# A small product pass whose first matmuls are cut in halves for two of four row tiles, and whose copies out of PSUM are cut in two

## The chip, the cores and the metric

The kernel runs on one core of a Trainium2 chip. The metric is the device time in microseconds of one execution, lower is better. TensorE (PE in the profile; PEld are its weight loads), VectorE (DVE), ScalarE (ACT), GpSimd (POOL) and the DMA queues run side by side and wait for each other through semaphores. TensorE writes its results into PSUM, which has eight banks of 512 float32 values per partition; VectorE and ScalarE read them there.

## The reference

All in float32, with a batch of 8, 4224 rows and 192 channels:

```python
w = softmax(weight, axis=-1)                    # 8 heads x 7 taps
y = sum over k of w[head, k] * x[s + k - 6]     # causal depthwise convolution, 24 channels a head
mu, var = mean and variance of y over its 192 channels
xn = (y - mu) / sqrt(var + 1e-6) * g_ln
out = y + relu(xn @ w_ch1) @ w_ch2              # 192 -> 768 -> 192
```

The scaling by 1/sqrt(var) is positive, so the kernel moves it behind both matmuls, and the subtraction of the mean and the factor g_ln are worked into `w_ch1` once.

## The kernel before

The rows are cut into 18 groups. A group is at most 128 partitions times 16 rows (`J` = 16). Groups 3 to 17 (15 of them) go through `up_mixed` (first matmul) and then `down_fast` (second matmul); the earlier, smaller ones take other paths that the change leaves as they are. Every engine's instructions are issued in the order in which the code stands (`tc.manual_schedule()`); the semaphore waits follow from the tiles that an instruction reads and writes.

The first matmul is a matrix product in Strassen's manner (Winograd's form): seven products of quarter matrices in place of eight. It is made in two passes, which split the hidden columns: `one` takes one of the three blocks of 128 columns in each half (`Pass(PAIR, FC, X, Y)`, the small pass, `self.n` = 1), `two` takes the other two (`self.n` = 2). Each pass makes the seven products in this order, alternating between two sets of four PSUM banks, X and Y: X, Y, X, Y, X, Y, X. Some products add to what the set already holds (`first=False`), and after most products the set is read out before the next product goes into it.

One product is made by `rows_of_tiles`. The transposed activations lie so that 32 partitions hold 32 channels of one of four row tiles `q` (`NQ` = 4). A matmul of tile `q` uses 32 rows of the array, `32q` to `32q+31`, with 128 weight columns and 256 moving columns (8 row indices `j` times 32), and writes bank `q` of the set. In the small pass a product is 3 channel blocks `c` times 4 tiles `q`: 12 matmuls, written `q` inside `c`. The trace holds two records for each float32 matmul, and as many for its weights, so a product of the small pass has 24 matmul records. Its set holds 4 banks with 256 columns each in use: a readout of it is a 128x1024 operation.

The readout of a set is `evict` (a copy by ScalarE, or a Relu for the last product) or `close`. `close` with a `part` copies the set into a spare place through `evict` and then has a DMA with addition (`add_by_dma`, issued on POOL) add it to its target. In the small pass the ScalarE reads out after each of the seven products: `evict` into `c11`, `close` into the spare `two.c12[:, 0:1]`, `evict` into `c21`, `evict` into `c22`, `close` into `two.c12[:, 1:2]`, `close` into `two.c22[:, 0:1]`, and the Relu into `c12`. Before the change each is one instruction (line 651). In the last group (17, `last`) `evict` already cuts it: ScalarE takes banks 0 and 1, VectorE banks 2 and 3 (lines 642 to 650).

Of the kernel before, what the change touches and what calls it, by code (L numbers as in the profile page):

```python
# [10 lines left out]
AF = mybir.ActivationFunctionType  # L11
# [5 lines left out]
def kernel(  # L17
# [29 lines left out]
    nc = tc.nc  # L47
# [4 lines left out]
    P = 128  # L52
    Q = 64
    C = 32
# [8 lines left out]
    NQ = P // C  # L63
# [20 lines left out]
    HJ = J // 2  # L84
# [35 lines left out]
    def take_bank():  # L120
        i = turn[0] % 8
        turn[0] = i + 1
        return all_banks[:, i]

    def take_set():
        i = (turn[0] + 3) // 4 * 4 % 8
        turn[0] = i + 4
        return all_banks[:, i : i + 4]
# [393 lines left out]
            return  # L522
        nc.scalar.activation(dst, src, AF.Relu)  # L523

    def rows_of_tiles(banks, left, right, first=True, last=True, split=False):


        chunks, w = right.shape[2] // P, left.shape[1] * left.shape[3]
        for c in range(left.shape[2]):
            for i in range(chunks):  # L530
                for q in range(NQ):
                    rows = slice(C * q, C * q + C)
                    nc.tensor.matmul(  # L533
                        banks[:, q, i * w : i * w + w], right[rows, c, P * i : P * i + P],
                        left[rows, :, c, :], start=(first and c == 0 and i == 0),
                        stop=(last and c == left.shape[2] - 1), skip_group_check=split,
                    )

    def between(g, f):

# [12 lines left out]
    def up(g):  # L553


        n = groups[g][2]
        hidden_tile(g)
        for f in range(NF):
            banks = take_set()
            rows_of_tiles(banks, yt[g][:, 0:n], w1[:, :, f * P : f * P + P])  # L560
            evict_up(g, f, banks[:, :, 0 : n * C])
            if g == 0 and f == 0:
                first_tap(1, heads=(0, H // 2))
            elif g == 0 and f == 1:
                copies_of_w1(1, [(q, 1) for q in range(NQ)])
                scale_power(words_2[2])
            elif g == 0 and f < 4:
                first_tap(1, heads=(2 * f, 2 * f + 2))
            between(g, f)
# [16 lines left out]
    def quarters_of_y(g):  # L586
        if width(g) == C:
            cuts = [(slice(HJ * h, HJ * h + HJ), slice(0, C)) for h in range(2)]
        else:
            cuts = [(slice(0, J), slice(T * h, T * h + T)) for h in range(2)]  # L590
        return [yt[g][:, js, CH * k : CH * k + CH, ts] for js, ts in cuts for k in range(2)]
# [19 lines left out]
    def up_mixed(g, ahead, pending):  # L611
# [3 lines left out]
        last = g + 1 == NG  # L615
# [3 lines left out]
        a11, a12, a21, a22 = quarters_of_y(g)  # L619
# [3 lines left out]
        class Pass:  # L623
# [6 lines left out]
                    for h in range(2)  # L630
                ]

            def product(self, to, left, right, first=True, end=True):
                rows_of_tiles(to, left, right, first, end, True)

            def seen(self, banks, f=None):
                src = banks[:, :, 0 : self.n * W] if f is None else banks[:, :, W * f : W * f + W]
# [2 lines left out]
            def evict(self, banks, dst, relu=False, f=None):  # L640
                src = self.seen(banks, f)
                if last and self.n == 1:
                    near, far = [[v[:, :, q : q + 2] for v in (dst, src)] for q in (0, 2)]
                    if relu:
                        nc.scalar.activation(*near, AF.Relu)
                        nc.vector.tensor_scalar_max(*far, 0.0)
                    else:
                        nc.scalar.copy(*near)
                        nc.vector.tensor_copy(*far)
                    return  # L650
                nc.scalar.activation(dst, src, AF.Relu) if relu else nc.scalar.copy(dst, src)  # L651

            def close(self, c, banks, part=None, f=None):

# [25 lines left out]
        X, Y = take_set(), take_set()  # L680
        one, two = Pass(PAIR, FC, X, Y), Pass(0, PAIR, Y, X)
        p = one
        p.product(X, a11, p.b11, True, False)
        p.evict(X, p.c11)
        p.product(Y, a12, p.b21)
        p.close(p.c11, Y, two.c12[:, 0:1])
# [14 lines left out]
        p = two  # L701
# [52 lines left out]
        if last:  # L754

            n = J - fast[g]
# [249 lines left out]
    for g in range(NG):  # L1006
        mixed, last = g in MIXED, g + 1 == NG
        if g + 2 < NG and g not in (1, 2, 3):
            load_x(g + 2)
        if mixed:  # L1010
            work = up_mixed(g, ahead(g), pending)
            pending = iter(())
        else:
            up(g)
            work = []
# [47 lines left out]
        if last:  # L1063
# [4 lines left out]
            for j in range(fast[g], groups[g][2]):  # L1068
                rows = take_bank()[:, 0:D]
# [36 lines left out]
```

## Time and profile before

| | |
|---|---|
| median of 3 runs | 957.89 us (957.74 to 960.14) |
| span of the profiled execution, first to last instruction | 954.6 us |
| PE busy | 946.8 us (99%) |
| DVE busy | 894.2 us (94%) |
| ACT busy | 694.8 us (73%) |
| POOL busy | 341.8 us (36%) |
| granted TensorE clock | 9 (90% or more) in all 40 slices |
| first matmul of a whole group to first matmul of its `down_fast` | 27.96 us in 12 of the 15 groups |

The time of an execution is a few microseconds longer than its span. A line of groups of instructions gives the source line, the engine, the operation, what it writes and reads, the tile shapes, the count, the busy time and the mean length of one, then the idle time of the engine in front of them and what ended it. A line of the timeline gives the start in us from the start of the span, the length of the stretch, and in brackets the idle time before it with its releaser. Matmul records are pipelined: their lengths overlap, so PE counts as busy even while the rate at which matmuls start has dropped.

### The profile page before, as it was taken

To read this page: it belongs to the slowest core of one execution; us is meant where nothing else is said; L and a number is where in the kernel's file an instruction comes from. 1 tells how busy PE (TensorE), PEld (TensorE's weight loads), DVE (VectorE), ACT (ScalarE), POOL (GpSimd) and SP (SyncE) were. 2 spreads that over 40 slices of the span, in tenths; PEclk is the share of its full clock that TensorE was granted. 3 is DMA by queue.
4 is the path that set the end of the run, shared out by engine and by line. 5 is a ranking of instruction groups with operands and counts; after the bars stand their busy time and mean duration, and the time that the engine had idled before them with its cause. 6 is when DMAs were issued, how large, how long until landed. Compare 5 with 4: busy or idle time off the path is not lost.

```text
span 954.6 us, 37896 instructions
## 1 busy us (share of the span) xinstructions
PE 946.8 (99%) x16858; PEld 734.5 (77%) x16858; DVE 894.2 (94%) x1496; ACT 694.8 (73%) x1166; POOL 341.8 (36%) x474
## 2 busy tenths in 40 slices
PE   8999999999999999999999999999999999999998
PEld 7998896877869687786958778695867769586787
DVE  8999999999999999999999999999999999999867
ACT  7764678596877959687796968779695877967362
POOL 1158422613145141533227141452316232261330
PEclk9999999999999999999999999999999999999999
DMA  8359589689696988979697897969889697778261
GB/s 206 111 151 218 110 233 269 122 188 226 130 273 131 251 158 185 221 130 278 126 252 152 199 215 128 277 133 249 158 198 206 124 275 134 174 135 141 40 122 68
DMA packets 39832, 169.34 MB, mean 177 GB/s; under 512 B 4469, under 2 KB 8182, under 8 KB 33655
## 3 DMA queue, kind: packets, MB, share of 16 engines
q0 software_dynamic: 32864, 106.77, 60.2%
q1 hardware_dynamic: 6800, 60.16, 17.4%
q8 instruction: 132, 2.16, 0.9%
q14 instruction: 30, 0.25, 0.1%
q10 hardware_dynamic: 6, 0.00, 0.0%
HBM read 38.93 MB, written 50.33 MB: 94 GB/s over the span
## 4 chain that ended last, share of the span: by engine, by line
PE 96%; DMA 1%; POOL 1%; ACT 1%; issue 0%; DVE 0%; ACTq 0%; POOLq 0%
PE ps L533 46%; PE ps L850 44%; PE ps L787 4%; PE ps L367 1%; DMA room<-room 1%; DMA out_dram<-y 1%; PE ps L326 1%; ACT room L651 0%; POOL room L609 0%; POOL d L460 0%; ACT y L380 0%; POOL r L483 0%; POOL d L478 0%; POOL d L479 0%; PE ps L335 0%
## 5 line engine op out<-in xcount | busy, mean ns | idle before, releaser
L417 DVE SCALAR_TENSOR_TENSOR y<-xg,taps,y 128x384 f32<-128x384 f32 (+3 forms) x720 | 364.8, 583 | 2.6 <-DMA y<-room 1.4
L850 PE MATMUL ps<-room,w2sums 128*32 128x256 f32 (+2 forms) x4608 | 246.6, 371 | 0.0
L533 PE MATMUL ps<-yt,w 32*128 32x256 f32 (+2 forms) x4104 | 234.7, 378 | 1.0 <-ACT room L523 0.5
L533 PEld LDWEIGHTS ps<-yt,w 32*128 32x128 f32 x4104 | 204.2, 185 | 26.3 <-issue 8.7
L651 ACT COPY room<-ps 128x1024 f32<-128x1024 f32 (+1 forms) x129 | 169.0, 1310 | 74.5 <-PE ps L533 73.5
L850 PEld LDWEIGHTS ps<-room,w2sums 128*32 128x32 f32 x4608 | 149.3, 110 | 91.5 <-ACT room L664 5.3
L850 PE MATMUL ps<-room,w 128*32 128x256 f32 (+2 forms) x3456 | 188.9, 371 | 0.0
L817 DVE TENSOR_TENSOR room<-room 128x1024 f32<-128x1024 f32 (+2 forms) x147 | 161.2, 1170 | 22.6 <-PE ps L850 16.0
L850 PEld LDWEIGHTS ps<-room,w 128*32 128x32 f32 x3456 | 110.7, 110 | 70.3 <-DVE room L657 5.0
L533 PE MATMUL ps<-ysums,w1sums 32*128 32x256 f32 x2160 | 124.9, 379 | 0.2 <-issue 0.2
L533 PEld LDWEIGHTS ps<-ysums,w1sums 32*128 32x128 f32 x2160 | 109.5, 185 | 10.5 <-ACT room L651 3.3
L940 POOL DMA_DIRECT2D out_dram<-ot x69 | 59.0, 942 | 155.6 <-ACT ot L929 102.5
L409 POOL DMA_DIRECT2D y<-tb x59 | 52.5, 1386 | 153.5 <-ACT room L856 110.1
L856 ACT COPY cs<-ps 128x256 f32<-128x256 f32 (+2 forms) x192 | 70.1, 367 | 45.2 <-PE ps L850 45.2
L664 ACT ACTIVATE room<-room 128x1024 f32<-128x1024 f32 (+1 forms) x89 | 92.5, 1072 | 1.7 <-DMA room<-parts_cs 0.9
L929 ACT ACTIVATE ot<-ot,r 128x192 f32<-128x192 f32 x224 | 90.9, 464 | 0.0
L380 ACT ACTIVATE y<-xg,taps 128x384 f32<-128x384 f32 (+3 forms) x141 | 73.0, 607 | 1.0 <-DMA out_dram<-y 0.7
L448 DVE BATCH_NORM_STATS2 st<-y 128x6 f32<-128x192 f32 x264 | 70.1, 344 | 0.0
L856 ACT COPY room<-ps 128x256 f32<-128x256 f32 (+2 forms) x96 | 35.5, 370 | 45.8 <-PE ps L850 43.8
L398 ACT ACTIVATE tb<-xg,taps 128x384 f32<-128x384 f32 (+1 forms) x120 | 66.1, 628 | 0.0
L533 PE MATMUL ps<-yt,w1sums 32*128 32x256 f32 x1080 | 65.2, 380 | 0.6 <-ACT room L651 0.6
L533 PE MATMUL ps<-ysums,w 32*128 32x256 f32 x1080 | 64.5, 376 | 0.0
(119 smaller groups left out, 924.8 us busy)
## 6 DMA issues: line engine op xcount, KB each, us to landing
xg<-in_x_dram SPq DMA_DIRECT2D x14, 2112.0 KB, 16.4
room<-room POOLq DMA_DIRECT2D x45, 512.0 KB, 5.1
out_dram<-ot POOLq DMA_DIRECT2D x59, 384.0 KB, 9.6
y<-tb POOLq DMA_DIRECT2D x58, 384.0 KB, 8.4
out_dram<-y SPq DMA_DIRECT2D x13, 1536.0 KB, 8.8
room<-parts_cs POOLq DMA_DIRECT2D x28, 512.0 KB, 6.7
room<-parts_tb POOLq DMA_DIRECT2D x14, 1024.0 KB, 7.6
xg<-in_x_dram POOLq DMA_DIRECT2D x1, 2112.0 KB, 13.8
```

What stands on the lines that cost most here:

```text
L380: nc.scalar.mul(y[g][:, 0:n, cs], xg[g][:, 0:n, cs], taps[:, h, 0:1])
L398: nc.scalar.mul(tb[g][:, 0:n, cs], xg[g][:, 1 : 1 + n, cs], taps[:, h, 1:2])
L417: nc.vector.scalar_tensor_tensor(out=y[g][:, 0:n, cs], in0=t[:, k : k + n, cs], scalar=taps[:, h, k : k + 1], in1=y[g][:, 0:n, cs], op0=AL ...
L448: nc.vector.bn_stats(out=sums[g][:, j, :], in_=y[g][:, j, :])
L533: nc.tensor.matmul(banks[:, q, i * w : i * w + w], right[rows, c, P * i : P * i + P], left[rows, :, c, :], start=(first and c == 0 and i = ...
L651: nc.scalar.activation(dst, src, AF.Relu) if relu else nc.scalar.copy(dst, src)
L664: nc.scalar.activation(c, c, AF.Relu)
L817: nc.vector.tensor_tensor(a[:, *dst, f], a[:, *left, f], a[:, *right, f], op=op)
L850: nc.tensor.matmul(dst[C * q : C * q + C, 0:w], right[:, f, C * c : C * c + C], left[:, f, q], start=(first and f == PAIR), stop=(f == PAI ...
L856: nc.scalar.copy(to[:, c], dst[:, 0:w].rearrange("p (j t) -> p j t", t=t))
L929: nc.scalar.mul(ots[g][:, j, :], ots[g][:, j, :], rstd[g][:, j : j + 1])
L940: nc.gpsimd.dma_start(out=rows[:, d0:d1], in_=src[:, d0:d1], accum_op=ALU.add)
```

## The change

In all groups from 3 on but the last, the first product of the small pass (`X`, from `a11`) is issued with `lead` = 4: for row tiles 0 and 1 a matmul over the first 4 of the 8 `j` (128 of 256 columns) of channel block 0 goes ahead of everything; then the loops run as before, with the tiles 0 and 1 of channel block 0 taking only the other 128 columns. Later channel blocks and products are issued as before. In the small pass each copy of a set that is not a Relu becomes two copies of two banks each (128x512 twice instead of 128x1024). The Relu copy, the large pass and the last group stay as they are.

```diff
-    def rows_of_tiles(banks, left, right, first=True, last=True, split=False):
+    def rows_of_tiles(banks, left, right, first=True, last=True, split=False, lead=0):
 
-        chunks, w = right.shape[2] // P, left.shape[1] * left.shape[3]
+        chunks, n, t = right.shape[2] // P, left.shape[1], left.shape[3]
+        w = n * t
+
+        def one(c, i, q, j1, j2, start):
+            rows = slice(C * q, C * q + C)
+            nc.tensor.matmul(
+                banks[:, q, i * w + j1 * t : i * w + j2 * t], right[rows, c, P * i : P * i + P],
+                left[rows, j1:j2, c, :], start=start,
+                stop=(last and c == left.shape[2] - 1), skip_group_check=split,
+            )
+
+        for q in range(NQ // 2 if lead else 0):
+            one(0, 0, q, 0, lead, first)
         for c in range(left.shape[2]):
             for i in range(chunks):
                 for q in range(NQ):
-                    rows = slice(C * q, C * q + C)
-                    nc.tensor.matmul(
-                        banks[:, q, i * w : i * w + w], right[rows, c, P * i : P * i + P],
-                        left[rows, :, c, :], start=(first and c == 0 and i == 0),
-                        stop=(last and c == left.shape[2] - 1), skip_group_check=split,
-                    )
+                    begun = lead if c == i == 0 and q < NQ // 2 else 0
+                    one(c, i, q, begun, n, first and c == 0 and i == 0 and not begun)
...
-                nc.scalar.activation(dst, src, AF.Relu) if relu else nc.scalar.copy(dst, src)
+                halves = [slice(0, 2), slice(2, NQ)] if self.n == 1 and not relu else [slice(0, NQ)]
+                for qs in halves:
+                    to, of = dst[:, :, qs], src[:, :, qs]
+                    nc.scalar.activation(to, of, AF.Relu) if relu else nc.scalar.copy(to, of)
...
-        p.product(X, a11, p.b11, True, False)
+        p.product(X, a11, p.b11, True, False, 0 if last else HJ // 2)
```

More of the change, by code (lines that the diff above doesn't have):

```diff
@@ L631, in __init__, with product @@
                 ]
-            def product(self, to, left, right, first=True, end=True):
-                rows_of_tiles(to, left, right, first, end, True)
+            def product(self, to, left, right, first=True, end=True, lead=0):
+                rows_of_tiles(to, left, right, first, end, True, lead)
             def seen(self, banks, f=None):
```

## The prediction

> **What bounds the kernel now.** I began with the page's first part and its chain of work: PE is never free.
>
> ```profile
> PE 946.8 (99%) x16858; PEld 734.5 (77%) x16858; DVE 894.2 (94%) x1496; ACT 694.8 (73%) x1166; POOL 341.8 (36%) x474
> ...
> PE 96%; DMA 1%; POOL 1%; ACT 1%; issue 0%; DVE 0%; ACTq 0%; POOLq 0%
> ```
>
> So only what lets matmuls start sooner can shorten the run, and the page cannot show where that is: records overlap, so a late start hides in a busy PE. The weight loads tell. Their timeline in the small pass of a whole group (the pass that begins at 228.41):
>
> ```profile
> 228.41 2.47 PEld L533 LDWEIGHTS ps<-yt,w 32*128 32x128 f32 x48 [0.41 <-issue]
> 231.12 1.18 PEld L533 LDWEIGHTS ps<-ysums,w1sums 32*128 32x128 f32 x24 [0.24 <-ACT room L651]
> 232.48 1.21 PEld L533 LDWEIGHTS ps<-ysums,w1sums 32*128 32x128 f32 x24 [0.18 <-issue]
> 233.83 1.18 PEld L533 LDWEIGHTS ps<-ysums,w 32*128 32x128 f32 x24
> 235.26 1.18 PEld L533 LDWEIGHTS ps<-yt,w1sums 32*128 32x128 f32 x24 [0.26 <-ACT room L651]
> 236.61 1.21 PEld L533 LDWEIGHTS ps<-yt,w 32*128 32x128 f32 x24 [0.17 <-issue]
> 238.03 2.04 PEld L533 LDWEIGHTS ps<-yt,w 32*128 32x128 f32 x40 [0.22 <-ACT room L651]
> ```
>
> From the third product on, the loads of nearly every product start after a pause, and where a releaser is named it is ScalarE's copy of line 651. What that costs, I read from the same seven products of the last group, whose readouts are already cut by bank pair (ScalarE one pair, VectorE the other). Timelines of PE, first the whole group, then the last group, from the pass's first matmul to a product in the middle of the large pass:
>
> ```profile
> 228.41 2.87 PE L533 MATMUL ps<-yt,w 32*128 32x256 f32 x48
> ...
> 243.31 1.90 PE L533 MATMUL ps<-ysums,w1sums 32*128 32x256 f32 x32
> ```
> ```profile
> 894.29 2.87 PE L533 MATMUL ps<-yt,w 32*128 32x256 f32 x48
> ...
> 899.58 1.47 PE L533 MATMUL ps<-ysums,w 32*128 32x256 f32 x24
> 900.87 1.47 PE L533 MATMUL ps<-yt,w1sums 32*128 32x256 f32 x24
> ...
> 908.64 2.55 PE L533 MATMUL ps<-ysums,w1sums 32*128 32x256 f32 x44
> ```
>
> 243.31 − 228.41 = 14.90 us against 908.64 − 894.29 = 14.35 us: **0.55 us are lost in a whole group's small pass.** 14 groups give 7.7 us, 0.8% of the run; that is all that can be won. The undisturbed pace is 900.87 − 899.58 = 1.29 us a product, six steps of 0.216 us in which the four row tiles each run one record.
>
> Why the pass loses it, from ScalarE's timeline in the same stretch:
>
> ```profile
> 230.06 1.01 ACT L651 COPY room<-ps 128x1024 f32<-128x1024 f32 x1 [1.14 <-PE ps L533]
> 231.35 1.01 ACT L651 COPY room<-ps 128x1024 f32<-128x1024 f32 x1 [0.28 <-PE ps L533]
> 232.77 1.01 ACT L651 COPY room<-ps 128x1024 f32<-128x1024 f32 x1 [0.40 <-PE ps L533]
> ```
>
> Call S the start of a product's last step. A record lasts 0.37 us (two products, 228.41 to 231.28) and the copy of the second starts 0.07 later, at 231.35: the copy starts at S + 0.44. It ends at S + 1.45, and the weights go in 0.05 later (231.07 to 231.12), at S + 1.51. The set is wanted again after one product on the other set, so its first matmul should run at S + 0.216 + 1.295 = S + 1.51, but the weights must come first: a tile's first load needs about 0.10 us that is otherwise hidden (after a pause a step takes 0.32 instead of 0.216). The pass is therefore 0.11 us too slow at every wait for a copy. ScalarE itself has room: it idles 0.3 to 0.5 us before every copy. It is the latency of one copy that binds.
>
> **The change, part by part.**
>
> *The copies.* Six copies of 128x1024 per group become twelve of 128x512, 84 more instructions. Both forms are in the trace:
>
> ```profile
> L651 ACT COPY room<-ps 128x1024 f32<-128x1024 f32 x84 | 85.1, 1013 | 42.2 <-PE ps L533 42.2
> L648 ACT COPY room<-ps 128x512 f32<-128x512 f32 x6 | 3.5, 586 | 4.7 <-PE ps L533 4.7
> ```
>
> Two halves take 2 × 0.586 = 1.17 us, unless they overlap. Back-to-back copies do: two of 128x1024 in one stretch take 1.93 us and not 2.03, 0.10 less. So the second half ends 0.586 − 0.10 + 0.586 = 1.07 us after the first begins, 0.06 later than the one copy did; without overlap 0.16 later. I take the overlap, since those two stand on the same engine, line and set. The pair fills 1.07 of each 1.295 us product, so the engine's queue does not run over.
>
> *The waits.* Tiles 0 and 1 now wait for the first half alone, ready at S + 0.44 + 0.59 + 0.05 = S + 1.08 against the S + 1.40 that would be in time: they never wait. Tiles 2 and 3 wait for the second half: S + 0.44 + 1.07 + 0.05 = S + 1.56, matmul at S + 1.67, wanted at S + 1.51. If all four tiles finish together, tiles 2 and 3 lose 0.16 us, once. From then on they run 0.16 us behind the other pair, so at the next sets the first half starts that much ahead of their own end, the second half finds itself in time (1.67 − 0.16 = 1.51), and nothing more is lost. Behind a tile-2 wait on PE's queue stand the next channel block's matmuls of tiles 0 and 1; these already have two records each, 0.43 us, in hand when the wait is reached, more than 0.16.
>
> *The lead.* Four short matmuls of 128 columns in place of two of 256: eight records and loads in place of four. The warm-up matmuls at the start, 128 columns with 128 weight columns, give their price: 28 records in 3.39 us, about 0.11 each, against 0.108 for half a step. Tiles 0 and 1 so lose 4 × 0.111 − 0.432 = 0.01 us, and they have time. What the lead does to tiles 2 and 3 depends on whether PE lets them past the four short matmuls that stand ahead of them. If it does, they start at once and lose the 0.16 us above; if it does not and holds them for two short records, they start 0.22 us late and lose nothing later (0.22 > 0.16). The nearest row says it does:
>
> ```profile
> 228.41 0.71 PE L533 MATMUL ps<-yt,w 32*128 32x256 f32 x8
> ```
>
> The narrower timeline (to 228.72) has only four records here, the next four follow 0.32 us after. Two records of one matmul cannot run in one tile at once, so these four are the first records of four tiles, and the second records, earlier in the program, were overtaken.
>
> The Trainium skill ("TensorE: Matmul & The Clock Gate", Part 3, "What overlaps and what doesn't") says the contrary: matmuls start in strict program order. By that rule tiles 2 and 3 would wait for the short records of tiles 0 and 1, the pass would lose about 0.45 us, and the sum would be near 956.5. The start of four tiles together speaks against it.
>
> *The rest, at nothing.* `close`'s DMA additions wait for the second half, 0.06 us more; they are read about ten us later (issued 232.67, the Relu on `c11` at 247.9). VectorE must keep up with a shorter group: it idles 0.86 us before line 657 until PE's product is done (253.99), more than the gain. Should that cover go, PE would wait at the `down_fast` that follows. SP's queue gets nothing new.
>
> **The sum.** Loss per pass after: 0.16 (tiles pass) to 0.22 (tiles held) us; the calculation for 0.16 closes without a margin, so I take 0.19. Gain 0.55 − 0.19 = 0.36 us × 14 = 5.0 us. The first of the 14 passes (117.20) has another stall of some 0.4 us in its fourth product with no copy behind it, which may swallow its share: −0.2. 4.8 us off the span of 954.6 gives 949.8; the median stands 3.3 above that span, so **953.1 us**. Bounds of the likeliest case: 0.10 us of loss gives 6.3 (951.6); no overlap of the halves, 0.26 of loss, gives 4.0 (953.9).
>
> **The rivals.**
>
> 1. *Slower: the pairs do not come apart.* If PE's queue, standing at tile 2's wait, also stops tiles 0 and 1, every set waits for the second half, which ends 0.06 (overlapped) to 0.16 us (not) later than the one copy, and the 0.22 us of the lead is paid on top. A wait that comes late for X leaves the next one, for Y, time to spare, so three of the six count: 0.22 + 3 × 0.16 = 0.70 us a pass, or 0.22 + 3 × 0.26 = 1.00, against 0.55: 0.15 to 0.45 us more, × 14 = 2.1 to 6.3 us, 960.0 to 964.2. It decides once the loss exceeds 0.55 us a pass. Against it: the overtaking above. For it: no row shows tiles 0.16 us apart.
> 2. *The lead is dear.* If short records cost a whole load (185 ns in the page's group of loads) and not 111, tiles 0 and 1 lose 4 × (0.185 − 0.108) = 0.31 us at once and, with the 0.16 of the other pair, the pass 0.47: gain 0.08 × 14 = 1.1 us, 956.8. The warm-up rows speak against it, but they used the whole array.
> 3. *No difference: the time comes back elsewhere*, by VectorE or a late DMA. Line 651 once waited 1.0 us for a DMA, and PE 0.62 at 750.66; one more such event costs 0.7, a few would eat most: 955.5 to 958.
>
> **How the numbers follow.** Forecast 0.62 (951.6 to 954.5), rival 1 0.17, rivals 2 and 3 0.09 each, larger gains 0.03. 0.3% is 2.9 us, about what a measurement of this kernel can tell from none. Faster: the forecast, larger gains and a little of rival 3, 0.66; same: rivals 2 and 3, 0.17; slower: rival 1, 0.17. The range 951.6 to 957.0 leaves out rival 1 and the tails.
>
> **What the changed profile would show.** Right: 168 copies of 128x512 with a mean near 586 in place of 84; pauses of the weight loads of line 533 gone except one per pass; 243.31 − 228.41 down from 14.90 to about 14.5; `up_mixed` at 27.6 us. Wrong: pauses at every second product (rival 1), a first product longer by 0.3 us (rival 2), or shorter passes with new PE waits on DVE or DMA (rival 3).

## The result, and the profile after

The changed kernel took 952.47 us (median of 5 runs, 950.92 to 953.63) against 957.89 us (by then the median of 5 runs, 956.61 to 960.14): a ratio of 0.9949, with a 95% interval of 0.9937 to 0.9961, so 5 us faster, between 3.7 and 6.0. Its profiled execution has a span of 951.4 us.

The weight loads in the small pass of a whole group (it begins at 229.14 here), in the timeline of PEld of the changed kernel; columns are start, length, engine, line, operation, count, and in brackets the idle time before:

```profile
229.14 2.48 PEld L533 LDWEIGHTS ps<-yt,w 32*128 32x128 f32 x52 [0.41 <-issue]
231.64 2.71 PEld L533 LDWEIGHTS ps<-ysums,w1sums 32*128 32x128 f32 x48
234.23 1.42 PEld L533 LDWEIGHTS ps<-ysums,w 32*128 32x128 f32 x24
235.52 1.47 PEld L533 LDWEIGHTS ps<-yt,w1sums 32*128 32x128 f32 x24
236.82 4.29 PEld L533 LDWEIGHTS ps<-yt,w 32*128 32x128 f32 x78
```

All the pauses from the third product on are gone; the one per pass that the prediction left is not to be seen, since the loads of tiles 0 and 1 go on while tiles 2 and 3 wait. The 52 in the first line are the 48 loads of two products and the four that the lead adds. In the table of waits over the whole span, the entry of line 533's loads for ScalarE's copies has gone with them. Before:

```profile
PEld ps L533 <- issue: 11.6, 44, 0.6
PEld ps L533 <- ACT room L651: 10.9, 43, 1.0
```

After (its first two lines; no line for the copies, now line 662, and line 533 follows):

```profile
PEld ps L533 <- issue: 7.0, 17, 0.7
PEld ps L861 <- DVE room L668: 5.3, 15, 0.7
```

The timeline of PE, from the pass's first matmul to the product in the middle of the large pass:

```profile
229.14 2.89 PE L533 MATMUL ps<-yt,w 32*128 32x128 f32 x52
231.85 2.90 PE L533 MATMUL ps<-ysums,w1sums 32*128 32x256 f32 x48
234.44 1.61 PE L533 MATMUL ps<-ysums,w 32*128 32x256 f32 x24
235.74 1.66 PE L533 MATMUL ps<-yt,w1sums 32*128 32x256 f32 x24
237.03 6.84 PE L533 MATMUL ps<-yt,w 32*128 32x256 f32 x120
243.50 2.75 PE L533 MATMUL ps<-ysums,w1sums 32*128 32x256 f32 x46
```

The form `32x128` in its first line is that of the short matmuls which open the pass. 243.50 − 229.14 = 14.36 us, against 14.90 before and 14.35 in the undisturbed last group. The starts belong to a product's first record, which is tile 0's: **tiles 0 and 1 lose nothing any more** but 0.01 us for the lead's short records. The lengths tell of the other pair. The product at 235.74 lasts 1.66 us where the last group's lasted 1.47: its last records, tiles 2 and 3, end 0.19 us later. The whole of `up_mixed` is as long as its slower pair: from the first matmul to the first of `down_fast` 27.61 us, against 27.96, in 12 of the 14 groups; in the last group, which the change does not touch, it is 27.57 in both.

ScalarE's timeline shows the new copies in pairs (the first three sets):

```profile
230.77 1.07 ACT L662 COPY room<-ps 128x512 f32<-128x512 f32 x2 [1.12 <-PE ps L533]
232.06 1.07 ACT L662 COPY room<-ps 128x512 f32<-128x512 f32 x2 [0.22 <-PE ps L533]
233.36 1.08 ACT L662 COPY room<-ps 128x512 f32<-128x512 f32 x2 [0.22 <-PE ps L533]
```

The two halves overlap by about 0.1 us and take 1.07 us, 0.06 more than the one copy's 1.01. ScalarE does more work, and the second half of a set ends 0.06 us later after the start of its readout than the one copy did; and yet the pass is faster.

### The profile page after: what moved, and what is told of

The parts are those of the page before. It is cut to its first block, busy times and chain, and to the rows that moved or that the text cites. A ratio compares the mean times of both kernels' runs of the same rounds, so it can differ in the third digit from the quotient of the medians.

```text
span 951.4 us, 38106 instructions
## 1 busy us (share of the span) xinstructions
PE 944.5 (99%) x16914; PEld 750.8 (79%) x16914; DVE 894.1 (94%) x1496; ACT 700.0 (74%) x1250; POOL 340.8 (36%) x474
## 4 chain that ended last, share of the span: by engine, by line
PE 67%; DVE 0%; issue 0%
PE ps L861 34%; PE ps L533 32%; PE ps L798 1%; DVE y L955 0%
## 5 line engine op out<-in xcount | busy, mean ns | idle before, releaser
L533 PE MATMUL ps<-yt,w 32*128 32x256 f32 (+2 forms) x4160 | 237.9, 373 | 0.3 <-DVE yt L428 0.3
L533 PEld LDWEIGHTS ps<-yt,w 32*128 32x128 f32 x4160 | 211.0, 185 | 21.6 <-issue 6.2
L861 PEld LDWEIGHTS ps<-room,w2sums 128*32 128x32 f32 x4608 | 151.4, 110 | 89.5 <-ACT room L675 4.6
L662 ACT COPY room<-ps 128x512 f32<-128x512 f32 (+1 forms) x213 | 174.2, 859 | 62.6 <-PE ps L533 62.6
L861 PEld LDWEIGHTS ps<-room,w 128*32 128x32 f32 x3456 | 112.9, 110 | 69.3 <-DVE room L668 5.3
L533 PE MATMUL ps<-ysums,w1sums 32*128 32x256 f32 x2160 | 127.2, 376 | 0.3 <-issue 0.3
L533 PEld LDWEIGHTS ps<-ysums,w1sums 32*128 32x128 f32 x2160 | 116.5, 185 | 5.3 <-issue 0.7
L533 PE MATMUL ps<-yt,w1sums 32*128 32x256 f32 x1080 | 69.2, 375 | 0.0
L533 PE MATMUL ps<-ysums,w 32*128 32x256 f32 x1080 | 68.5, 374 | 0.0
```

Of the source, the lines that this page charges most:

```text
L533: nc.tensor.matmul(banks[:, q, i * w + j1 * t : i * w + j2 * t], right[rows, c, P * i : P * i + P], left[rows, j1:j2, c, :], start=start, ...
L662: nc.scalar.activation(to, of, AF.Relu) if relu else nc.scalar.copy(to, of)
L861: nc.tensor.matmul(dst[C * q : C * q + C, 0:w], right[:, f, C * c : C * c + C], left[:, f, q], start=(first and f == PAIR), stop=(f == PAI ...
```

## Experiments

The theory: the copy of a whole set is 0.1 us too slow for PE at every set. Cut in two, tiles 0 and 1 are never late; tiles 2 and 3 fall behind once, and from then on their own later finish gives the second half its time. The lead plays no part, because PE lets tiles 2 and 3 overtake. The rivals: the lead sets the pairs apart; two short copies gain by themselves; a wait for a second half is paid at every set.

The measure for all runs is the stretch from the first matmul of a whole group to its first in `down_fast`, the same to 0.01 us in nearly every group of a run (27.96 before, 27.61 after); the times of a run go with it. Ratios are to the kernel before, on the same chip, where its median was 957.41 us beside the first four experiments and 957.34 beside the last four.

### The changed kernel again

> The changed kernel as it is, beside the experiments on the same chip. Expected: ratio to the kernel before 0.995 (0.9937 to 0.9961 was measured), 27.61 us from the first matmul of a whole group to the first of its down_fast. The few stalls of 0.2 to 0.4 us without a wait that its first profile had in three down_fast stretches should stand elsewhere or be gone, if they are chance; in the same places if they come with the program.

952.34 us, ratio 0.995 (0.9938 to 0.9962), stretch 27.61. The stalls are taken up in the last section.

### Cut copies without the lead

```diff
-        p.product(X, a11, p.b11, True, False, 0 if last else HJ // 2)
+        p.product(X, a11, p.b11, True, False)
```

> Copies cut in two, no lead. Theory (the pairs come apart by themselves at the first wait for a second half, since row tiles overtake each other; the lead does nothing): the same stretch of 27.60 to 27.63 us and a ratio to the kernel before equal to that of the changed kernel within 0.001; tiles 2 and 3 fall 0.14 to 0.16 us behind in the third product. Rival (the lead is what sets the pairs apart): without it each wait for a second half holds everything, 27.8 to 28.0 us, ratio 0.999 to 1.001.

951.35 us, ratio 0.994 (0.9928 to 0.9952), stretch 27.60. PE's timeline of this kernel:

```profile
228.97 2.87 PE L533 MATMUL ps<-yt,w 32*128 32x256 f32 x48
231.66 2.90 PE L533 MATMUL ps<-ysums,w1sums 32*128 32x256 f32 x48
234.25 1.61 PE L533 MATMUL ps<-ysums,w 32*128 32x256 f32 x24
235.55 1.66 PE L533 MATMUL ps<-yt,w1sums 32*128 32x256 f32 x24
```

The first two products take 2.87 us, as before the change, and all four tiles start together. The third and fourth already take 2.90, the fifth and sixth 1.61 and 1.66: the same figures as with the lead. In the single records tiles 2 and 3 fall 0.14 us behind in the third product and another 0.05 in the sixth, where ScalarE's first copy of that set comes 0.05 us late. So the pairs come apart without the lead, and the rival that it sets them apart falls. The stretch is 0.014 us shorter, the price of four short records (4 × 0.111 − 0.432 = 0.012).

In the first of the 14 groups the lead costs more: 28.43 us with it and 28.18 without. That pass has a stall for which the profile names no wait, in its third product and after 63 matmul records of the pass with the lead and without it, so four records earlier in the product with it. Before the change:

```profile
119.91 1.14 PE L533 MATMUL ps<-ysums,w1sums 32*128 32x256 f32 x15
121.24 2.10 PE L533 MATMUL ps<-ysums,w1sums 32*128 32x256 f32 x33 [0.19 <-issue]
```

After:

```profile
120.97 1.02 PE L533 MATMUL ps<-ysums,w1sums 32*128 32x256 f32 x11
122.31 2.21 PE L533 MATMUL ps<-ysums,w1sums 32*128 32x256 f32 x35 [0.32 <-issue]
```

Without the lead the pause is 0.17 us, again after 48 + 15 records. What makes the stall is not shown. Over 14 groups the lead so costs 13 × 0.014 + 0.24 = 0.4 us; the medians differ by 1.0, but the intervals overlap, so I claim only the 0.4.

### The lead without cut copies

```diff
-                halves = [slice(0, 2), slice(2, NQ)] if self.n == 1 and not relu else [slice(0, NQ)]
+                halves = [slice(0, NQ)]
```

> The lead, with copies in one piece. Theory: every set is still waited for whole, 27.96 us a stretch plus at most 0.02, ratio 1.000 to 1.0005. Rival (the lead lets the copy start sooner): a copy in one piece waits for tile 3, so a lead that held tiles 2 and 3 back would show as 0.2 us more, 28.15 us, ratio 1.003; a gain is expected by no theory.

957.92 us, ratio 1.0006 (0.9996 to 1.0016), stretch 27.97: 0.015 us more, the short records' price again. Tiles 2 and 3 were not held. Only the first group pays more here too, 28.73 us against 28.38 before.

### The halves in the other order

```diff
-                halves = [slice(0, 2), slice(2, NQ)] if self.n == 1 and not relu else [slice(0, NQ)]
+                halves = [slice(2, NQ), slice(0, 2)] if self.n == 1 and not relu else [slice(0, NQ)]
```

> As the changed kernel, but of each two copies the one of banks 2 and 3 goes first. Theory (the gain needs the pairs to come apart, and PE's queue is in order at a wait): the first wait in program order is now tile 0's, for the later copy, and it holds tiles 2 and 3 too although theirs is ready; all tiles wait for the second copy, 0.06 us later than the one copy of before: 27.95 to 28.1 us a stretch, ratio 0.9995 to 1.002. Rival (two short copies gain by themselves, whichever is first, or PE's queue passes the waiting tile): 27.6 us, ratio 0.995.

961.04 us, ratio 1.0036 (1.0023 to 1.0049), stretch 28.21. The same work in the same pieces is now slower than the kernel before. PEld's timeline:

```profile
230.18 2.48 PEld L533 LDWEIGHTS ps<-yt,w 32*128 32x128 f32 x52 [0.41 <-issue]
232.96 1.18 PEld L533 LDWEIGHTS ps<-ysums,w1sums 32*128 32x128 f32 x24 [0.30 <-ACT room L662]
234.37 1.21 PEld L533 LDWEIGHTS ps<-ysums,w1sums 32*128 32x128 f32 x24 [0.24 <-issue]
235.73 1.18 PEld L533 LDWEIGHTS ps<-ysums,w 32*128 32x128 f32 x24 [0.15 <-ACT room L662]
237.22 1.18 PEld L533 LDWEIGHTS ps<-yt,w1sums 32*128 32x128 f32 x24 [0.31 <-ACT room L662]
```

The pauses are back, and longer (0.30 and 0.31 where they were 0.24 and 0.26). The wait that stands first in PE's queue is tile 0's, for the later copy; tiles 2 and 3, whose copy is done 0.5 us earlier, stand behind it and do not get past. That is what the prediction's slower rival would have been: 0.80 us lost in a pass, within the 0.70 to 1.00 priced for it, though made up otherwise. Of the 0.22 that the rival charged for the lead only 0.015 is paid, and the later end of the copy is paid in four products where it counted three sets. The time came out above the range expected for this run, since I had reckoned that only alternate sets pay the extra 0.06. Against the lead alone (same lead, whole copies), the starts of the third, fourth, sixth and eighth products slip by 0.04 to 0.06 each, 0.24 in all. Short copies alone gain nothing.

### A pause between the halves

```diff
+    pause = consts.tile([P, 2, 64], F32, name="pause")
+    nc.gpsimd.memset(pause, 0.0)
...
                     nc.scalar.activation(to, of, AF.Relu) if relu else nc.scalar.copy(to, of)
+                    if len(halves) == 2 and qs.start == 0:
+                        nc.scalar.copy(pause[:, 1], pause[:, 0])
```

Both are built on the cut copies without the lead; the second kernel has 160 in place of 64.

> As the kernel with cut copies and no lead (27.60 us a stretch), with a 128x64 copy of ScalarE, of its own data, between the two halves: the second half comes about 0.11 us later in every set (a copy of 64 columns should take 0.21 us, 0.10 of it overlapped). Theory (tiles 2 and 3 fall behind once and stay there, so the delay is paid once a pass): 27.70 to 27.74 us, ratio to the kernel before 0.9955 to 0.9965. Rival (every wait for a second half is paid, and tiles 0 and 1 are held with it): 6 x 0.11 more, 28.2 us, ratio 1.003.

> The same with a 128x160 copy between the halves: the second half comes about 0.19 us later, and tiles 2 and 3 should be some 0.38 us behind in the end. Theory: still paid once, 27.78 to 27.82 us, ratio 0.997 to 0.998, as long as the lag stays under the two records, 0.43 us, that tiles 0 and 1 have in hand, and ScalarE's 1.26 us a product stay under 1.295. Rival: paid at every set, 28.7 us, ratio 1.012.

The first took 952.22 us, ratio 0.9945 (0.9928 to 0.9961), stretch 27.69; the second 954.02 us, 0.9966 (0.9953 to 0.9979), stretch 27.77. ScalarE's timeline of the second:

```profile
229.66 0.59 ACT L664 COPY room<-ps 128x512 f32<-128x512 f32 x1 [1.10 <-PE ps L535]
230.15 0.33 ACT L666 COPY pause<-pause 128x160 f32<-128x160 f32 x1
230.37 1.17 ACT L664 COPY room<-ps 128x512 f32<-128x512 f32 x2
231.44 0.33 ACT L666 COPY pause<-pause 128x160 f32<-128x160 f32 x1
231.67 1.17 ACT L664 COPY room<-ps 128x512 f32<-128x512 f32 x2
```

The second half starts 0.71 us after the first (229.66, and 230.37 as the first of the next two), not 0.48: ScalarE runs without a gap, and every second half of six comes 0.23 us later. The stretch grew by 0.17, not by 1.4. With 64 columns the halves are 0.63 apart, 0.15 later, and the stretch grew by 0.09. **The delay is paid once in a pass.** Both delays are larger than was expected, and both stretches and ratios lie a little below their expected ranges: each stretch grew by 0.06 less than its delay. The 0.05 us that the plain cut loses in its sixth product is not lost again when the lag is already larger, as the next lines show. In the second kernel the lag is so long that the timeline of PE separates the pairs by itself:

```profile
233.34 0.38 PE L535 MATMUL ps<-ysums,w 32*128 32x256 f32 x2
233.50 0.38 PE L535 MATMUL ps<-ysums,w1sums 32*128 32x256 f32 x2
```

At 233.34 two records of the fifth product start (tiles 0 and 1), and after them, at 233.50, two more of the fourth (tiles 2 and 3): one step and 0.16 us behind, 0.37 us. Two products later, after the sixth, the same pairs start at 235.93 and 236.09: the lag has not grown.

### Three banks and one

```diff
-                halves = [slice(0, 2), slice(2, NQ)] if self.n == 1 and not relu else [slice(0, NQ)]
+                halves = [slice(0, 3), slice(3, NQ)] if self.n == 1 and not relu else [slice(0, NQ)]
```

It is also without the lead.

> As the kernel with cut copies and no lead, but cut into banks 0 to 2 and bank 3 (128x768 and 128x256). Theory (what the last tile loses is set by the sum of the two copies, which is the same: 0.80 + 0.37 against 2 x 0.586): 27.59 to 27.62 us a stretch, with tile 3 alone 0.2 us behind, ratio 0.994. Rival (what counts is how early the first part is ready): 0.21 us later for three of the tiles, 27.7 to 27.9 us.

951.94 us, ratio 0.9947 (0.9932 to 0.9962), stretch 27.61. The two copies took 0.80 and 0.38 us, the same sum as two halves, and the stretch is the same: between these two places of the cut, the place does not matter.

### The pairs apart in the first product

```diff
-        for q in range(NQ // 2 if lead else 0):
-            one(0, 0, q, 0, lead, first)
-        for c in range(left.shape[2]):
-            for i in range(chunks):
-                for q in range(NQ):
-                    begun = lead if c == i == 0 and q < NQ // 2 else 0
-                    one(c, i, q, begun, n, first and c == 0 and i == 0 and not begun)
+        pairs = [(0, 1), (2, 3)] if lead else [range(NQ)]
+        for pair in pairs:
+            for c in range(left.shape[2]):
+                for i in range(chunks):
+                    for q in pair:
+                        one(c, i, q, 0, n, first and c == 0 and i == 0)
```

> As the changed kernel, but in the first product all six matmuls of tiles 0 and 1 stand ahead of the six of tiles 2 and 3, whole, with no short ones. It asks how far a matmul of another tile may overtake. Theory (tiles 2 and 3 pass whatever stands ahead for other tiles): the four tiles still start within 0.1 us of each other, 27.60 to 27.65 us a stretch, ratio 0.994 to 0.995. Rival (a tile holds only a few matmuls, and the queue stops behind a full tile): tiles 2 and 3 start up to 5 x 0.216 = 1.08 us late, 28.5 to 28.7 us, ratio 1.008 to 1.012.

956.66 us, ratio 0.9994 (0.9984 to 1.0003), stretch 27.94: in neither of the two ranges that were expected. In narrow windows of PEld's timeline two weight loads have begun by 227.55, six by 228.04 and ten by 228.06. The first two are those of tiles 0 and 1 at 227.50, and the last four to come include the first loads of tiles 2 and 3, 0.55 us late:

```profile
227.50 0.52 PEld L533 LDWEIGHTS ps<-yt,w 32*128 32x128 f32 x6 [0.41 <-issue]
```
```profile
227.50 0.74 PEld L533 LDWEIGHTS ps<-yt,w 32*128 32x128 f32 x10 [0.41 <-issue]
```

They start when the third records of tiles 0 and 1 do, so when six of the twelve records ahead of them have started. Nothing is lost after that: the lag stays at 0.55, and 27.60 − 0.20 + 0.55 = 27.95 is 0.01 from what was measured. This is what a real lead would have cost: all of the gain.

## Why the prediction was right

953.1 us was forecast, 952.47 came, and the sign, the mechanism and most terms hold.

- *What the pass loses (0.55 us).* Right. Tiles 0 and 1 won 0.54 of it back (14.90 to 14.36).
- *The copies (second half 0.06 us later).* Right: 1.07 us a pair.
- *The waits (0.16 us, once).* Right in kind, shown by the two pauses. The lag came in two parts, 0.14 and 0.05; the calculation closed without a margin, as the prediction said. 0.19 was taken and 0.20 measured (0.55 − 0.35).
- *The lead (tiles 2 and 3 start at once).* Right, and shown by the runs with and without it; its price was as said in every group but the first, where it was 0.24 to 0.35 us and not 0.01. The rule weighed in the prediction, from the Trainium skill ("TensorE: Matmul & The Clock Gate", Part 3, "What overlaps and what doesn't"), that matmuls start strictly in program order, does not hold here: with eight records of other tiles ahead, tiles 2 and 3 started within 0.03 us of tile 0 in the changed kernel. It is not without a bound either, as twelve ahead held them for 0.55 us.
- *The sum.* 0.345 us in each of 12 groups, where 0.36 was taken. The first pass gained nothing (28.43 after 28.38), where half its share was left in: its stall stands in the third product, not in the fourth as the prediction read it, and the lead made it dearer; without the lead the pass gained 0.20. One group (from 284.68) lost its gain to VectorE, which waited 1.37 us for the DMA addition of the second tap; that is the third rival, once, and the second profile of the same kernel does not have it. So the passes explain 4.1 us in the first profile and 4.4 in the second, under the forecast's 4.8, while the two sets of runs moved by 5.4 and 5.1, with intervals that reach down to 3.6. That the forecast time came so near is thus partly luck: about 1 us of the difference is not traced. In the profiled pair a stretch longer by 0.9 us behind a late DMA (PE's wait at 750.66 before) was absent after, but at the same place ScalarE waits for that DMA again in the kernel without the lead (0.33 us, at 745.04), whose stretch there is 27.83: the cut does not remove such waits.
- *The base.* The span of 954.6 was taken as 3.3 us under the median. In the runs of the changed kernel, time and span differ by 2.1 to 2.2 us; if it is the same before, the profiled execution there was a quicker one than the median. It did not enter the difference.
- *What the profile would show.* `up_mixed` at 27.6 and 168 copies of 589 ns came as said. The other mark, 14.90 down to about 14.5, was badly chosen: it times tile 0, which loses nothing, and it fell to 14.36.

The best version of all runs is the cut copies without the lead, in the traces by 0.014 us in a usual group and 0.24 in the first.

## What to carry to other kernels

Where a matmul waits for a readout that is only a little too slow, as here by 0.1 us, it is worth trying to cut the readout by bank groups, so that the tiles that own them can fall into step with their own copies; the extra time of the cut was then paid once and not at every set. In this kernel it worked only with the part copied first whose matmuls stand first in PE's queue: the other order made it slower than the one without the cut. A product's first record tells of the fastest tile; the end of a stage tells of the slowest, and only that is won.

## What the runs showed that was not expected

PE let row tiles overtake others that stand ahead in the program, but not without limit. With eight records ahead (the lead), tiles 2 and 3 started 0.03 us after tile 0; with twelve, 0.55 us after it. In both cases six of those ahead had not started yet. No run lies between, and whether records or their loads are counted was not tried.

In the changed kernel's first profile three `down_fast` stretches took 27.82 to 27.93 us in place of 27.42, with gaps of 0.2 to 0.4 us between matmuls for which the profile names no wait: 1.4 us in one execution. Two of the gaps lie in the first and the last of these windows (columns: the window and its length, busy us and instruction counts of PE, PEld, DVE, ACT and POOL, granted clock, DMA share, GB/s):

```profile
281.00:282.50 1.50, 1.50 (x30) 0.72 (x25) 1.50 (x6) 0.37 (x1) 1.04 (x2) 1.00 1.07 212
282.50:284.00 1.50, 1.50 (x36) 0.88 (x30) 1.50 (x7) 0.37 (x1) 1.42 (x2) 1.00 1.09 209
...
497.00:499.00 2.00, 2.00 (x37) 1.20 (x33) 2.00 (x3) 2.00 (x6) 0.00 (x0) 1.00 1.09 307
```

The first has 30 matmul records where the even pace of the second gives 36. The clock is full, and the DMA share is above 1, but it is so in the second window too, which has no gap. In the second profile of the same kernel the same three stretches took 27.60, 27.87 and 27.46, so such gaps come at the same places but not at the same size. The other kernels have them too, and larger. The longest `down_fast` of a whole group took 27.62 us before the change, 27.81 without the lead, 27.67 with three banks and one, 28.21 and 28.23 with the pauses, and 28.50 with the pairs apart. With the lead alone and with the halves in the other order it is the last group's that is long, 21.42 and 22.16 us where it is 20.73 before and after; in the latter it holds the largest gap of all ("issue": the profile shows nothing that PE waited for):

```profile
928.60 1.65 PE L861 MATMUL ps<-room,w 128*32 128x192 f32 x33 [1.21 <-issue]
```

So the gaps do not come with the change, and a profiled execution carries between 0.2 and almost 2 us of them. A difference of 1 us between medians of a few runs therefore says little by itself here; the stretch through `up_mixed`, which leaves them out, says more. What holds PE there stays open.
